# A head pair's block transpositions in its predecessor's fourth step, and one tile for the last keys' weights and inverses

## The chip, the cores and the metric

The kernel runs on one core of a Trainium2 chip. The metric is the device time of one execution in microseconds. Before the change three executions took 1657.55, 1662.69 and 1664.34 us; the median is 1662.69 us. The profile shows one execution with a span of 1655.7 us on the core.

## What is computed

Two blocks follow each other, all in fp32, for 8 batches of 576 tokens. The first is attention with 8 heads of 64 dimensions, in which only scores within tau of their row's maximum count:

```python
scores = scale * np.matmul(q, k.transpose(0, 1, 3, 2))
thresh = np.max(scores, axis=-1, keepdims=True) - tau
scores = np.where(scores >= thresh, scores, -1000000000.0)
attn = np.exp(scores - np.max(scores, axis=-1, keepdims=True))
attn = attn / (np.sum(attn, axis=-1, keepdims=True) + 1e-09)
out = np.matmul(attn, v)
```

The heads are then put side by side (576 x 512 for each batch), and the second block mixes and widens them:

```python
mixed = np.real(np.fft.fft(np.fft.fft(x, axis=1), axis=2))
u = x + mixed
un = (u - mean(u)) / np.sqrt(var(u) + 1e-06)
return u + np.maximum(un @ w_ch1, 0.0) @ w_ch2
```

The two channel weights (512 x 2048 and 2048 x 512) come as 64-bit floats and are converted to fp32 inside the kernel.

## The kernel before, in words

**Steps.** The attention works on pairs of heads, 4 pairs in each of 8 batches, so 32 pairs. A pair takes five steps (t = 0 to 4). In steps 0 to 3 both heads' scores for 128 queries are computed (`scores`, line 430, two score tiles of two PSUM banks each). In the fifth step (t = 4) the last 64 queries of both heads are done together from a block-diagonal tile `q_ends` (line 436), so that only one score tile is used. There are two buffers of score tiles in all. `softmax` then takes the maximum on VectorE (L453), the exponential on ScalarE (L461), and the masking with its sum on VectorE (L469), which is the last reader of a score tile. In the first two batches the weights are not normalized: `rec` holds the inverse of each sum, spread over 128 columns by GpSimd (L493).

**Weights transposed.** In the next step `transposed_weights` brings the previous step's weights to keys by queries: TensorE transposes them into PSUM (L533 the last 64 keys of both heads, L536 the inverses, both into one bank `pe`; L552 the other keys into `pw`), and ScalarE copies them out (L540 and L544 for `pe`, L554 and L556 for `pw`). The last keys' weights go to the tile `ends`, the inverses to the tile `recs`. `weighted_values` multiplies with v (L581) and, in the first two batches, with the inverses on VectorE (L589). For pairs whose heads are taken in reverse, GpSimd writes a reversed v (`v_rev`, L522 and L528) first.

**Preparing a pair.** q and k are loaded in 32-column pieces. `scale_q` (L390, GpSimd) scales q in place, and `prep_pair` transposes 32 by 32 blocks on VectorE: k (L401), a piece of k (L402) and q (L404), into `kT` (two buffers) and `qT` (one buffer), then issues the loads of the pair after it. `prep_ends` (L413, GpSimd) copies the last 64 queries from `qT` to `q_ends` at t = 1, so that after the scores of t = 3 nobody reads `qT` any more.

**Three stages of the program.** The order on the engines in the first two is the order in which the code is written.

- Batch 0 (`step`, 20 steps, until about 135 us): attention alone, beside the conversion of the first channel weight, whose passes lie on VectorE (L297, L300, L313), ScalarE (L305, L308, L311) and GpSimd (L318, L319). `busy` lets TensorE multiply dummy tiles.
- Batch 1 (`second_batch`, 20 steps, about 135 to 315 us): attention of batch 1, the conversion of the second channel weight, the Fourier mixing of batch 0 (the additions into `u_t`, L723 and L727) and the first channel products (L814 and L840), which `fill` puts between the attention's matmuls. `advance` runs the conversion's stages.
- Batches 2 to 7 (the last loop, from about 315 us): only TensorE's order is as written; a planner orders the other engines. Here `prep_pair` already stands at t = 3, and weights are normalized before they are transposed, so there are no inverses.

In the first two stages `prep_pair(n + 1)` stands at t = 4, after the softmax of that step. In `second_batch`, `prep_ends` and `scale_q` stand ahead of the mixing and of the transposed weights.

Of the kernel before, what the change touches and what calls it, by code (L numbers as in the profile page):

```python
# [9 lines left out]
FP32 = mybir.dt.float32  # L10
INT32 = mybir.dt.int32
UINT32 = mybir.dt.uint32
ALU = mybir.AluOpType
# [34 lines left out]
def kernel(  # L48
# [12 lines left out]
    nc = tc.nc  # L61
    B, H, S, D = q.shape
# [4 lines left out]
    NT = 5  # L67
# [341 lines left out]
    def prep_ends(n):  # L409

        for j in range(2):
            hp = slice(64 * j, 64 * j + 64)
            nc.gpsimd.tensor_copy(q_ends[hp, hp], heads[n][0][hp, 512:S])  # L413
# [90 lines left out]
    def weights_in_parts(i):  # L504

        n, t = divmod(i, NT)
        e, rec = steps.pop(i)
        if t in (0, 2):

            e_t = sb.tile([128, 8, S - 256], FP32, tag="e_t", bufs=1, name="e_t")
            ends = sb.tile([128, S - 256], FP32, tag="ends", bufs=1, name="ends")
            recs = None
            if rec is not None:
                recs = sb.tile([128, S - 256], FP32, tag="sums", bufs=1, name="recs")
            vt = heads[n][2]
            if t == 0 and PAIRS[n % NPAIR] % 2:

                vt = sb.tile([128, 10, D], FP32, tag="vr", bufs=1, name="v_rev")  # L520
                src = heads[n][2]
                nc.gpsimd.tensor_copy(vt[:, :, 0:1], src[:, :, 0:1])  # L522
                last = src[:, :, D - 1 : D]
                down = bass.AP(
                    tensor=last.tensor, offset=last.offset,
                    ap=[list(last.ap[0]), list(last.ap[1]), [-1, D - 1]],
                )
                nc.gpsimd.tensor_copy(vt[:, :, 1:D], down)  # L528
            heads[n] = (*heads[n][0:2], vt, e_t, ends, recs)
        e_t, ends, recs = heads[n][3:6]  # L530
        q0 = 128 * (t - (0 if t < 2 else 2))
        pe = ps.tile([128, 4, 128], FP32, tag="mm", bufs=4, name="pe")
        nc.tensor.transpose(pe[:, 0, :], e[:, 512:640], ident[:, :])  # L533
        kept = [ends]
        if rec is not None:
            nc.tensor.transpose(pe[:, 1, :], rec[:, :], ident[:, :])  # L536
            kept.append(recs)
        for c, dst in enumerate(kept):
            if t < 4:
                nc.scalar.copy(dst[:, q0 : q0 + 128], pe[:, c, :])  # L540
            else:
                for j in range(2):
                    hp = slice(64 * j, 64 * j + 64)
                    nc.scalar.copy(dst[hp, q0 : q0 + 64], pe[hp, c, hp])  # L544
        qs = slice(q0, q0 + (128 if t < 4 else 64))
        for j in range(2 if t < 4 else 1):
            pw = ps.tile([128, 4, 128], FP32, tag="mm", bufs=4, name="pw")
            if j == 1:
                yield
            for c in range(4):  # L550
                c0 = (S + D) * j + 128 * c
                nc.tensor.transpose(pw[:, c, :], e[:, c0 : c0 + 128], ident[:, :])  # L552
            if t < 4:
                nc.scalar.copy(e_t[:, 4 * j : 4 * j + 4, qs], pw[:, :, :])  # L554
            else:
                nc.scalar.copy(  # L556
                    e_t[:, :, qs].rearrange("p (j c) q -> p j c q", j=2),
                    pw[:, :, :].rearrange("p c (j q) -> p j c q", j=2),
                )

    def weighted_values(n, part):

        b, p = n // NPAIR, PAIRS[n % NPAIR]
        _, _, vt, e_t, ends, recs = heads[n]
        m = (256, S - 256)[part]
        if n % NPAIR == 0 and part == 0:

            xs[b] = [None] * NPAIR
            x = xs[b][p] = sb.tile([128, m], FP32, tag="half", bufs=1, name="x_first")
        else:  # L570
            x = xs[b][p]
            if x is None or n % NPAIR == 0:
                x = sb.tile([128, S], FP32, tag=f"x{p}", bufs=1, name=f"x{p}")
            if n % NPAIR == 0:
                nc.gpsimd.tensor_copy(x[:, 0:256], xs[b][p][:, :])
            xs[b][p] = x
        cols = slice(256 * part, 256 * part + m)
        pv = ps.tile([128, 512], FP32, tag="mm", bufs=4, name="pv")
        for c in range(5):
            for j in range(2):  # L580
                nc.tensor.matmul(  # L581
                    pv[64 * j : 64 * j + 64, 0:m], vt[:, 2 * c + j, :],
                    e_t[:, 4 * j + c, 0:m] if c < 4 else ends[:, 0:m],
                    start=(c == 0), stop=(c == 4), skip_group_check=True,
                )
        if normalized(n):
            nc.scalar.copy(x[:, cols], pv[:, 0:m])  # L587
        else:
            nc.vector.tensor_tensor(  # L589
                out=x[:, cols], in0=pv[:, 0:m], in1=recs[:, 0:m], op=ALU.mult  # L590
            )
        if part == 0:
            return
        heads.pop(n)
        if p % 2:

            swap = sb.tile([2, S], FP32, tag="half", bufs=1, name="swap")
            for j in range(2):
                nc.sync.dma_start(out=swap[j : j + 1, :], in_=x[64 * j : 64 * j + 1, :])
            for j in range(2):  # L600
                nc.sync.dma_start(out=x[64 * j : 64 * j + 1, :], in_=swap[1 - j : 2 - j, :])
# [575 lines left out]
    def step(i):  # L1177

        n, t = divmod(i, NT)
        scores(i)  # L1180

        def last_stages():
            run = chunks.pop(i - 1, None)
            for _ in range(2 if run else 0):
                next(run, None)

        if t == 1 and n > 0:
            softmax(i, lambda: weighted_values(n - 1, 1), last_stages)
            load_v(n + 1)
        elif t == 3:  # L1190
            softmax(i, lambda: weighted_values(n, 0), last_stages)
        else:
            softmax(i, None, last_stages)
        if t == 1 and n > 0:
            pass
        elif later and later[0][0] <= i:
            later.pop(0)[1](i)
        else:
            busy(2 if i < NCHUNK else 1)
        if t == 2:  # L1200
            scale_q(n + 1)
        if t == NT - 1:
            prep_pair(n + 1)
        if t == 1:
            prep_ends(n)
        if i in chunks:
            next(chunks[i])
        if i > 0:
            transposed_weights(i - 1)
        if i in chunks:  # L1210
            next(chunks[i])
        while after and after[0][0] <= i:
            after.pop(0)[1]()
        if i > 0 and i + 3 < NCHUNK:
            chunks[i + 3] = w1_chunk(i + 3)
        if t == 2 and n > 0:
            folds.append(fold_rows(n - 1))
        if folds and next(folds[0], True):
            folds.pop(0)
# [93 lines left out]
    def second_batch(i):  # L1313
# [10 lines left out]
        chunks.pop(first - 1, None)  # L1324
        transfers(first)
        fold_more()
        if t == 1:
            prep_ends(n)
        if t == 2:
            scale_q(n + 1)  # L1330
        if first == 0:
            weighted_values(n - 1, 1)
            scores(i + 1)
            column_means(LAST)
            copy_mean(LAST)
            folds.append(fold_rows(n - 1))
            while folds:
                fold_more()
            load_v(n + 1)
            start_batch(0)  # L1340
            mix(3)
            mix(3)
        elif first == 1:
            mix(3)
            transposed_weights(i - 1)
            mix(2)
            mirrored(LAST)
            for c, eng in ((1, nc.vector), (3, nc.vector), (0, nc.gpsimd), (2, nc.gpsimd)):
                less_mean(eng, LAST, c)
            advance(first)  # L1350
            advance(first)
        elif first == 2:
            mix(2)
            transposed_weights(i - 1)
            mix(2)
            weighted_values(n, 0)
            advance(first)
            advance(first)
        else:
            fill()  # L1360
            transposed_weights(i - 1)
            advance(first)
            advance(first)
            fill()
            if t == 4:
                prep_pair(n + 1)
            fill()
            if t == 2:
                weighted_values(n, 0)
            if t == 0:  # L1370
                weighted_values(n - 1, 1)
                folds.append(fold_rows(n - 1))
                load_v(n + 1)
        if first == 16:
            fold_halves(1)
        if first < 3:
# [96 lines left out]
```

## Time and profile before

| what | value |
|---|---|
| median of three executions | 1662.69 us |
| span in the profile | 1655.7 us |
| transposition of q (L404), 32 times | 0.76 to 0.78 us each |
| copies of `ends` and `recs`, 128 x 128 (L540), mean until 315 us | 0.264 and 0.273 us |
| copies of 64 x 64 (L544), mean until 315 us | 0.20 and 0.21 us |
| scaling of q on GpSimd (L390) around 210 to 300 us | 1.72 to 1.73 us |

The table's durations are those of single instructions, as the trace's groups and timelines give them. What a duration costs depends on whether another engine stands still meanwhile. In the lines of the profile, PE is TensorE, PEld its weight loads, DVE VectorE, ACT ScalarE, POOL GpSimd. A timeline's line has the start in us, the length in us, the engine, the line of the kernel, the operation, what it writes and reads, and how many instructions are merged in it; the square bracket at the end tells how long the engine stood idle before it and which instruction ended that. In the list of groups the columns are busy time, mean time of one in ns, and idle time before them with its main releaser.

### The profile page before, as it was taken

Reading aid. Unit: us, or ns where it says so; the run is one execution under the profiler, and the core shown is the slowest. Engines: PE = TensorE matmul, PEld = TensorE weight load, DVE = VectorE, ACT = ScalarE, POOL = GpSimd, SP = SyncE. Lnnn points to the kernel's source line nnn. Section 1 sums busy time; section 2 is a strip of 40 time slices with the busy share of each in tenths; the row PEclk is TensorE's granted clock in tenths of the full one; section 3 lists DMA queues with packets and bytes.
Section 4 is the critical chain, followed back from the end, with each engine's and each line's share of the span. In section 5 each row is a group of like instructions: output and inputs, shape, how many; then the busy total and the mean of one; then the engine's idle time right before and its main releaser. Section 6 shows DMA issues by size and latency. Waiting matters only on the chain.

```text
span 1655.7 us, 27993 instructions
## 1 busy us (share of the span) xinstructions
PE 1584.1 (96%) x10346; PEld 1248.7 (75%) x10346; DVE 1170.7 (71%) x2518; ACT 820.9 (50%) x1786; POOL 660.1 (40%) x875
## 2 busy tenths in 40 slices
PE   8888878999999999999999999999999999999998
PEld 4545445557888787878888778887888788889998
DVE  7986776667768678776676768787786868664444
ACT  5764566444535464645353556454646455532111
POOL 6773565141431525225333253424342244215232
PEclk9999989999999999999999999999999999999999
DMA  6423221211011111100101010111101110000000
GB/s 158 122 55 111 56 83 42 43 28 29 12 35 20 25 26 29 36 16 21 28 16 35 15 35 16 42 22 22 29 15 43 22 28 1 14 4 11 13 14 14
DMA packets 203086, 57.43 MB, mean 35 GB/s; under 512 B 193827, under 2 KB 193829, under 8 KB 202950
## 3 DMA queue, kind: packets, MB, share of 16 engines
q1 hardware_dynamic: 200438, 55.34, 14.2%
q8 instruction: 82, 1.34, 0.3%
q10 hardware_dynamic: 2512, 0.30, 0.1%
q14 instruction: 54, 0.44, 0.1%
HBM read 46.02 MB, written 9.44 MB: 33 GB/s over the span
## 4 chain that ended last, share of the span: by engine, by line
PE 77%; DVE 14%; ACT 5%; issue 2%; POOL 1%; DVEq 0%; ACTq 0%; POOLq 0%
PE ph L918 23%; PE po L1082 20%; PE pv L581 9%; PE sc L430 8%; PE pw L552 5%; PE po L840 3%; DVE e L469 3%; DVE neg L453 2%; PE ph L814 2%; ACT e L461 2%; PE sc L436 1%; PE py L684 1%; PE pn L774 1%; PE pa L701 1%; DVE hs L1043 1%
## 5 line engine op out<-in xcount | busy, mean ns | idle before, releaser
L453 DVE TENSOR_REDUCE neg<-sc 128x1 f32<-128x576 f32 x288 | 207.5, 749 | 174.2 <-PE sc L430 159.9
L461 ACT ACTIVATE e<-sc,neg 128x576 f32<-128x576 f32 x288 | 212.2, 737 | 229.1 <-DVE neg L453 228.7
L469 DVE SCALAR_TENSOR_TENSOR e<-sc,thr,e 128x576 f32<-128x576 f32 x288 | 229.5, 813 | 50.5 <-ACT thr L465 49.0
L1082 PE MATMUL po<-w,hs 128*128 128x256 f32 x1024 | 246.9, 384 | 0.0
L1082 PEld LDWEIGHTS po<-w,hs 128*128 128x128 f32 x1024 | 186.7, 191 | 33.9 <-issue 12.9
L430 PE MATMUL sc<-kT,qT 64*128 64x288 f32 x1024 | 169.3, 434 | 35.0 <-DVE qT L404 27.7
L918 PE MATMUL ph<-u_t,w 128*128 128x128 f32 x1536 | 187.0, 276 | 0.0
L918 PEld LDWEIGHTS ph<-u_t,w 128*128 128x128 f32 x1536 | 179.1, 192 | 5.0 <-issue 3.7
L552 PE MATMUL pw<-ident,e 128*128 128x128 f32 x1152 | 171.2, 276 | 8.0 <-ACT y_o L689 2.3
L554 ACT COPY e_t<-pw 128x512 f32<-128x512 f32 x256 | 148.7, 594 | 49.8 <-PE pw L552 49.5
L430 PEld LDWEIGHTS sc<-kT,qT 64*128 64x128 f32 x1024 | 93.8, 188 | 98.3 <-issue 35.2
L552 PEld LDWEIGHTS pw<-ident,e 128*128 128x128 f32 x1152 | 135.7, 142 | 27.3 <-issue 4.2
L927 DVE TENSOR_TENSOR hs<-ph,hs 128x512 f32<-128x512 f32 x160 | 106.9, 685 | 69.5 <-PE ph L918 53.8
L918 PE MATMUL ph<-t_u,s_w 128*128 128x128 f32 x1024 | 126.4, 277 | 2.2 <-POOL t_u L892 1.8
L918 PEld LDWEIGHTS ph<-t_u,s_w 128*128 128x128 f32 x1024 | 119.5, 192 | 7.7 <-issue 4.9
L1082 PE MATMUL po<-hs,s_tile 128*128 128x256 f32 x512 | 121.5, 381 | 0.0
L796 DVE SCALAR_TENSOR_TENSOR u<-po,rstd,u 128x256 f32<-128x256 f32 (+1 forms) x164 | 75.3, 483 | 63.9 <-PE po L1082 62.9
L488 ACT ACTIVATE e<-e,den 128x576 f32<-128x576 f32 x96 | 74.5, 776 | 75.7 <-DVE den L481 75.3
L1082 PEld LDWEIGHTS po<-hs,s_tile 128*128 128x128 f32 x512 | 94.1, 190 | 13.7 <-issue 2.5
L935 ACT ACTIVATE hs<-hs 128x512 f32<-128x512 f32 x112 | 69.2, 630 | 62.1 <-DVE hs L927 62.1
L614 POOL TENSOR_TENSOR half<-x 128x287 f32<-128x287 f32 x48 | 40.5, 865 | 115.6 <-ACT x L587 61.0
L1078 POOL TENSOR_TENSOR hs<-hs,s_tile 128x512 f32<-128x512 f32 x32 | 42.1, 1318 | 109.4 <-PE po L1082 86.5
(196 smaller groups left out, 2911.2 us busy)
## 6 DMA issues: line engine op xcount, KB each, us to landing
hs<-in_moe_w_ch_dram SPq DMA_DIRECT2D x23, 512.0 KB, 4.5
q_in<-in_q_dram SPq DMA_DIRECT2D x128, 72.0 KB, 2.4
out_dram<-u SPq DMA_DIRECT2D x36, 256.0 KB, 2.1
k_in<-in_k_dram SPq DMA_DIRECT2D x124, 72.0 KB, 2.3
v_in<-in_v_dram SPq DMA_DIRECT2D x64, 128.0 KB, 2.3
w<-in_moe_w_ch_dram SPq DMA_DIRECT2D x6, 512.0 KB, 3.7
stage<-in_moe_w_ch_dram SPq DMA_DIRECT2D x3, 512.0 KB, 3.5
v_in<-in_v_dram SPq DMA_DIRECT2D x64, 16.0 KB, 2.1
```

The source lines that it names most:

```text
L430: nc.tensor.matmul(sc[j][:, c, 0:HALF], qT[hp, 128 * t : 128 * t + 128], kT[hp, k0 + HALF * c : k0 + HALF * (c + 1)], start=True, stop=True,)
L453: nc.vector.tensor_reduce(out=neg[:, j : j + 1], in_=sc[j][:, :, 0:HALF], axis=AXIS_XY, op=ALU.max, negate=True,)
L461: nc.scalar.activation(out=ej, in_=sc[j][:, :, 0:HALF], func=ACT.Exp, bias=neg[:, j : j + 1], scale=1.0)
L469: nc.vector.scalar_tensor_tensor(out=ej, in0=sc[j][:, :, 0:HALF], scalar=thr[:, j : j + 1], in1=ej, op0=ALU.is_ge, op1=ALU.mult, accum_out ...
L488: nc.scalar.activation(out=e[:, S : 2 * S], in_=e[:, S : 2 * S], func=ACT.Copy, scale=den[:, 1:2])
L552: nc.tensor.transpose(pw[:, c, :], e[:, c0 : c0 + 128], ident[:, :])
L554: nc.scalar.copy(e_t[:, 4 * j : 4 * j + 4, qs], pw[:, :, :])
L581: nc.tensor.matmul(pv[64 * j : 64 * j + 64, 0:m], vt[:, 2 * c + j, :], e_t[:, 4 * j + c, 0:m] if c < 4 else ends[:, 0:m], start=(c == 0), ...
L796: nc.vector.scalar_tensor_tensor(out=u, in0=product, scalar=self.rstd[:, t : t + 1], in1=u, op0=ALU.mult, op1=ALU.add,)
L918: nc.tensor.matmul(banks[name][:, 128 * q : 128 * q + 128], left[c][:, 512 * part + 128 * q : 512 * part + 128 * q + 128], right[c], start ...
L927: nc.vector.tensor_tensor(out=to, in0=bank, in1=to if other is None else other, op=ALU.add)
L1082: nc.tensor.matmul(bank[:, 0 : DM // 2], left[p], right[p], start=start and p == 0, stop=p == NK - 1, skip_group_check=True,)
```

## The change

Three things are changed, and only the first two batches are touched by name.

- `prep_pair(n + 1)` stands at t = 3 instead of t = 4, in `step` and in `second_batch`. Its purpose is to have the next pair's q and k in place before the pair's last step ends. The loads that it issues move with it.
- In `second_batch`, `prep_ends` and `scale_q` stand at the end of a step instead of its middle, behind what the same step puts on GpSimd.
- `ends` gets a second half that takes the place of `recs`. One ScalarE copy takes both from the bank `pe`: 128 x 256 elements for t < 4, two of 64 x 128 for t = 4. The tile `recs` had shared its buffer with a sum tile of the channel products; it is gone. Where there are no inverses, the copy is as before.

```diff
-            ends = sb.tile([128, S - 256], FP32, tag="ends", bufs=1, name="ends")
-            recs = None
-            if rec is not None:
-                recs = sb.tile([128, S - 256], FP32, tag="sums", bufs=1, name="recs")
+            ends = sb.tile([128, 2, S - 256], FP32, tag="ends", bufs=1, name="ends")
...
-        kept = [ends]
+        kept = 1
         if rec is not None:
             nc.tensor.transpose(pe[:, 1, :], rec[:, :], ident[:, :])
-            kept.append(recs)
-        for c, dst in enumerate(kept):
-            if t < 4:
-                nc.scalar.copy(dst[:, q0 : q0 + 128], pe[:, c, :])
-            else:
-                for j in range(2):
-                    hp = slice(64 * j, 64 * j + 64)
-                    nc.scalar.copy(dst[hp, q0 : q0 + 64], pe[hp, c, hp])
+            kept = 2
+        if t < 4:
+            nc.scalar.copy(ends[:, 0:kept, q0 : q0 + 128], pe[:, 0:kept, :])
+        else:
+            for j in range(2):
+                hp = slice(64 * j, 64 * j + 64)
+                nc.scalar.copy(ends[hp, 0:kept, q0 : q0 + 64], pe[hp, 0:kept, hp])
...
@@ step
-        if t == NT - 1:
+        if t == 3:
             prep_pair(n + 1)
...
@@ second_batch
-        if t == 1:
-            prep_ends(n)
-        if t == 2:
-            scale_q(n + 1)
         if first == 0:
             weighted_values(n - 1, 1)
...
-            if t == 4:
+            if t == 3:
                 prep_pair(n + 1)
...
+        if t == 1:
+            prep_ends(n)
+        if t == 2:
+            scale_q(n + 1)
         if first == 16:
             fold_halves(1)
```

More of the change, by code (lines that the diff above doesn't have):

```diff
@@ L528, in weights_in_parts @@
                 nc.gpsimd.tensor_copy(vt[:, :, 1:D], down)
-            heads[n] = (*heads[n][0:2], vt, e_t, ends, recs)
-        e_t, ends, recs = heads[n][3:6]
+            heads[n] = (*heads[n][0:2], vt, e_t, ends)
+        e_t, ends = heads[n][3:5]
         q0 = 128 * (t - (0 if t < 2 else 2))
@@ L563, in weighted_values @@
         b, p = n // NPAIR, PAIRS[n % NPAIR]
-        _, _, vt, e_t, ends, recs = heads[n]
+        _, _, vt, e_t, ends = heads[n]
         m = (256, S - 256)[part]
@@ L582, in weighted_values @@
                     pv[64 * j : 64 * j + 64, 0:m], vt[:, 2 * c + j, :],
-                    e_t[:, 4 * j + c, 0:m] if c < 4 else ends[:, 0:m],
+                    e_t[:, 4 * j + c, 0:m] if c < 4 else ends[:, 0, 0:m],
                     start=(c == 0), stop=(c == 4), skip_group_check=True,
@@ L589, in weighted_values @@
             nc.vector.tensor_tensor(
-                out=x[:, cols], in0=pv[:, 0:m], in1=recs[:, 0:m], op=ALU.mult
+                out=x[:, cols], in0=pv[:, 0:m], in1=ends[:, 1, 0:m], op=ALU.mult
             )
```

## The prediction

> **What bounds the kernel now.** I read the page's busy times and slices first, then the table of stretches, then who waits for the transposition of q, then each boundary between two pairs in the timeline.
>
> ```profile
> span 1655.7 us, 27993 instructions
> ...
> PE 1584.1 (96%) x10346; PEld 1248.7 (75%) x10346; DVE 1170.7 (71%) x2518; ACT 820.9 (50%) x1786; POOL 660.1 (40%) x875
> ...
> PE   8888878999999999999999999999999999999998
> ...
> L430 PE MATMUL sc<-kT,qT 64*128 64x288 f32 x1024 | 169.3, 434 | 35.0 <-DVE qT L404 27.7
> ```
>
> TensorE is 96% busy, but slices 1 to 7 (some 290 us) are not full. The row of the scores names the largest wait of TensorE in the page: 27.7 us, all put down to the transposition of q.
>
> ```profile
> 0.00:135.00 135.00, 113.76 (x562) 64.72 (x562) 110.94 (x251) 88.35 (x197) 94.81 (x155) 0.98 0.41 105
> 135.00:315.00 180.00, 151.83 (x763) 90.97 (x764) 125.95 (x280) 99.44 (x229) 89.96 (x112) 0.93 0.27 72
> 315.00:1656.00 1341.00, 1318.52 (x9022) 1092.98 (x9020) 933.82 (x1988) 633.14 (x1361) 475.33 (x608) 1.00 0.10 23
> ```
>
> Columns after the length: TensorE, its weight loads, VectorE, ScalarE, GpSimd, granted clock. Up to 135 us (batch 0 of the attention) VectorE is at 111 of 135 us, TensorE partly runs dummy products. From 135 to 315 us (batch 1) TensorE idles 28 us and its clock is 0.93. After 315 us it is 98% busy, so what is won before 315 us should move the end one for one.
>
> ```profile
> 221.15 1.04 PE L552 MATMUL pw<-ident,e 128*128 128x128 f32 x8
> 230.66 2.29 PE L430 MATMUL sc<-kT,qT 64*128 64x288 f32 x8 [8.47 <-DVE qT L404]
> 232.88 4.51 PE L814 MATMUL ph<-u_t,w 128*128 128x384 f32 x8
> ...
> 223.99 0.82 DVE L469 SCALAR_TENSOR_TENSOR e<-sc,thr,e 128x576 f32<-128x576 f32 x1 [1.30 <-ACT thr L465]
> ...
> 228.79 0.77 DVE L401 STREAM_TRANSPOSE kT<-k_in 128x576 f32<-128x576 f32 x1
> 229.57 0.24 DVE L402 STREAM_TRANSPOSE kT<-k_in 64x64 f32<-64x64 f32 x1
> 229.82 0.78 DVE L404 STREAM_TRANSPOSE qT<-q_in 128x576 f32<-128x576 f32 x1
> ```
>
> The longest of the eight waits, in batch 1. TensorE is done at 222.19 us and can't start the next pair's scores until the transpositions end at 230.60, though the fifth step's masking (L469), the other thing it needs for a free score bank, ended at 224.8. Two integer passes of the weight conversion (L297, L300) stand between. Afterwards TensorE runs at about half speed (x8 of L814 take 4.51 instead of 2.75 us).
>
> ```profile
> 70.32 1.24 PE L430 MATMUL sc<-kT,qT 64*128 64x288 f32 x8 [2.96 <-DVE qT L404]
> ...
> 70.19 1.08 DVE L297 TENSOR_SCALAR w<-hs 128x512 int32<-128x512 int32 x1
> ...
> 164.84 1.92 POOL L390 TENSOR_SCALAR q_in<-q_in,q_scale 128x576 f32<-128x576 f32 x1
> ...
> 171.61 2.93 PE L814 MATMUL ph<-u_t,w 128*128 128x384 f32 x4 [3.59 <-POOL u_t L727]
> ```
>
> First row pair: in batch 0 VectorE goes straight on to L297, so TensorE's wait is not the bound there. Second pair: scaling q stands on GpSimd ahead of the six additions that make u_t, for which TensorE waits 3.59 us.
>
> [...] the transpositions above stand behind the conversion's passes, whose result TensorE doesn't need. [...] after the waits of 8.47, 3.59 and 3.35 us the clock was half, after 2.88 and 2.52 us it was not, after 3.03 and 0.83 us close together it was. [...] L300, one shape, takes 0.41 to 1.52 us; I treat it as noise of 1 us.
>
> **The change, part by part.**
>
> 1. *Transpositions in the fourth step instead of the fifth, eight pairs.* One set takes 0.77 + 0.24 + 0.78 = 1.79 us of VectorE in either place. Removed: the wait of the scores on them. What then ends last is L469 of the fifth step (it frees the second score bank). Added: 1.79 us on VectorE ahead of the fifth step's maximum (L453), its exponential and that same L469, unless VectorE was idle there.
>  - Batch 0, boundaries at 39.4, 70.3, 101.4 us: VectorE has no gap in the fourth step, L453 moves by 1.8 us, L469 too; the fifth step gets 1.8 us back. Left over is TensorE's head start: the scores' end before L453, some 0.2 to 0.3 us each. Sum 0.7.
>  - 132.27: VectorE idle 1.11 us before the fifth step's L453, so it moves by 0.73; L469 ends at 130.6 instead of 129.9, scores start there: gain 1.6. The values' products behind it wait for ScalarE's copies (item 2): 0.4 more. They run at half speed now (4.54 and 1.17 us against 2.37 and 0.71 in the next pair: 2.6 us lost); the wait falls from 3.03 to 1.5 us; I take half of 2.6. Sum 3.3.
>  - 185.94: VectorE was idle 5.28 us in the fourth step, cost nothing; L469 had ended at 182.0, TensorE was free at 183.06: the 2.88 us vanish for TensorE, 2.2 for ScalarE, which has a ReLU ending at 185.8 ahead of the exponential. I take 2.2.
>  - 230.66: L453 moves by 1.75, but the exponential waited for ScalarE until 222.97, so L469 moves by 0.5 and ends at 225.3: gain 5.3. Half speed cost 1.05 (2.29 against 1.24) and 1.76 (4.51 against 2.75); TensorE still idles 3.1 us, so I take only a quarter, 0.7. Sum 6.0.
>  - 270.60: the transpositions queue behind a reciprocal that waits until 263.69; L453 ends 1.8 later, the exponential was held by a table load until 265.34, so L469 moves by 1.0 and scores start at 268.3: 2.3. The idleness falls from 3.35 to 1.1 us, half speed goes (1.05 + about 0.3): 1.3. Sum 3.6.
>  - 305.04: VectorE was idle 1.67 us; L453 moves by 0.2, scores from 305.04 to 303.0. Sum 2.0.
> 2. *One copy for two.* 32 pairs of 128x128 copies (0.264 and 0.273 us) become 32 of 128x256. The 128x512 copy takes 0.60, so by straight line one takes 0.37; two back to back take 0.43 from start to end. Gain 0.06 each, hidden mostly behind the waits of ScalarE for L453 (35.4 us in batch 1). In the fifth step's copies four of 64x64 (0.86 us from 42.96 to 43.82) become two: 0.4 each, on the path only at 132 us (counted above). The joint copy now waits for the reader of the inverses as well (L589; 2.6 us in four cases already wait so for the second copy, right behind the first), so nothing new waits long.
> 3. *Scaling q and the small q copies go later on GpSimd, batch 1.* At 171.61 u_t comes 1.92 - 0.52 (the two L413 copies, which now lie in the same busy stretch) = 1.4 us earlier; half speed after it (x4 in 2.93 us; at the 2.75 us for x8 it would be 1.4) costs 1.5, of which I take 1.0. Sum 2.4. At 209.73 TensorE waits 1.86 us for v_rev behind L413: 0.5. q is still ready: scaled at about 172, transposed from 173.2; later pairs 259.7 against 263.8 and 295.2 against 298.
> 4. *Loads of q and k issued a step earlier.* Nothing waits for them in batch 1; nothing gained.
> 5. *After step 40* TensorE's order is unchanged and VectorE's moves in a few places near 320 us; cost none, within 1 us.
>
> Sum: 0.7 + 3.3 + 2.2 + 6.0 + 3.6 + 2.0 + 2.4 + 0.5 = 20.7. 1662.7 - 20.7 = 1642.0 us. Ends of it: without any clock recovered and each boundary 10 to 15% worse, 14 us (1649); with all half speed recovered and the 2.9 us whole, 26 us (1637).
>
> **The rivals.**
> - *The wait only moves* (12%): batch 1 acts like batch 0, L469 or the conversion behind it takes the place of the transpositions, and a third of item 1's boundaries after 132 us stays (13.4 / 3 = 4.5), with 0.7, 1.4 and 0.5: 7 us, 1655.5. For it: VectorE is 70% busy in batch 1 and the first three boundaries. Against it: its idle gaps of 5.28, 1.67 and 1.25 us just where the transpositions go.
> - *More than counted* (8%): all waits of batch 1 and all half speed go: 0.7 + 3.0 + 2.6 + 3.4 + 2.9 + 0.5 + 8.2 + 2.8 + 3.3 + 1.4 + 2.5 = 31 us, 1631. For it: the loads and the conversion run ahead. Against it: L469 of the fifth step at 224.8.
> - *Slower* (2%): the fifth step's L453 moves by 1.79 in seven boundaries, nothing comes back, and the different order after step 40 costs a little: 1662.7 + 12.5 = 1675. Only if the scores then waited for something I don't see.
>
> **How the numbers follow.** 78% for the forecast, 12, 8 and 2 for the rivals. The measurements of before spread from 1657.6 to 1664.3, so 3 us of the range are theirs. 80%: 1633 to 1652. Faster by over 0.5% is under 1654.4: the forecast, the second rival, and half of the first: 0.91; same 0.07; slower 0.02.
>
> **What would show it.** The row of L430 should lose "DVE qT L404" and wait for L469, some 5 us in all; the stretch from 135 us shorter by about 20; its clock 0.96 or more; the wait of L814 for u_t about 2.2 us. It is wrong if L453 of the fifth step now waits on the transpositions in batch 1 and TensorE's scores come no earlier, or if the stretch after 315 us is no longer of the same length.

## The result and the profile after

| | before | after |
|---|---|---|
| median of the executions | 1662.79 us (1657.55 to 1664.34, 4 executions) | 1635.03 us (1634.93 to 1635.14, 4 executions) |
| the profiled execution | 1657.55 us, span 1655.7 us | 1634.93 us, span 1632.8 us |

The ratio of the times is 0.9839, 95% interval 0.9817 to 0.9860: the changed kernel is faster by 27.8 us of the medians. In two later series, each with both kernels on one chip, the medians differ by 24.1 us (1659.84 and 1635.78 us) and by 26.5 us (1662.40 and 1635.86 us). The two profiled executions differ by only 22.6 us, which matters below.

The page of the changed kernel, its head, TensorE's 40 slices and the row of the scores:

```profile
span 1632.8 us, 27899 instructions
...
PE 1583.2 (97%) x10346; PEld 1247.7 (76%) x10346; DVE 1170.1 (72%) x2518; ACT 816.0 (50%) x1738; POOL 661.2 (40%) x875
...
PE   8998889999999999999999999999999999999998
...
L430 PE MATMUL sc<-kT,qT 64*128 64x288 f32 x1024 | 174.1, 433 | 11.0 <-DVE e L469 9.9
```

TensorE has the same 10346 products and the same busy time to 1 us; what went is idleness. The row of the scores has lost "DVE qT L404 27.7", and what releases it most is now L469, the masking that frees a score tile. ScalarE has 48 instructions fewer: the 32 pairs of copies became 32, and 32 small ones 16.

The same three stretches as before (length, then TensorE, its weight loads, VectorE, ScalarE, GpSimd, granted clock):

```profile
0.00:135.00 135.00, 121.45 (x584) 67.97 (x586) 109.82 (x258) 87.70 (x176) 95.83 (x155) 0.96 0.45 114
135.00:315.00 180.00, 164.85 (x848) 98.54 (x848) 141.60 (x312) 107.91 (x228) 89.69 (x112) 0.99 0.27 69
315.00:1632.00 1317.00, 1296.93 (x8919) 1081.14 (x8916) 918.70 (x1949) 620.35 (x1334) 475.64 (x608) 1.00 0.10 23
```

In the second row TensorE's idleness fell from 28.2 to 15.2 us and its clock rose from 0.93 to 0.99. In the first its clock fell from 0.98 to 0.96; whether the change has a price in batch 0 is taken up below. After 315 us fewer products are left, since the attention runs ahead.

Who TensorE waits for from 135 to 315 us (total, times, longest), some rows of before and then of the changed kernel:

```profile
PE sc L430 <- DVE qT L404: 17.2, 4, 8.5
...
PE ph L814 <- POOL u_t L727: 3.6, 1, 3.6
```

```profile
PE sc L430 <- DVE e L469: 2.6, 3, 1.9
PE ph L810 <- POOL u_t L723: 2.1, 1, 2.1
...
PE pv L577 <- POOL v_rev L525: 1.5, 1, 1.5
```

The transposition of q has fallen below these rows (0.9 us in two waits in all until 315 us); before, 17.2 of its 27.7 us lay in this stretch. The four pairs' steps from 132.3 us on (128.1 us in the changed kernel) take 18.7 us less than before, where the prediction looked for about 20. The boundary with the wait of 8.47 us now looks like this (timeline, TensorE, then VectorE):

```profile
209.35 1.04 PE L548 MATMUL pw<-ident,e 128*128 128x128 f32 x8
211.12 0.75 PE L430 MATMUL sc<-kT,qT 64*128 64x288 f32 x2 [0.73 <-DVE qT L404]
213.79 2.17 PE L430 MATMUL sc<-kT,qT 64*128 64x288 f32 x6 [1.92 <-DVE e L469]
215.89 3.53 PE L810 MATMUL ph<-u_t,w 128*128 128x384 f32 x8
...
210.29 0.78 DVE L404 STREAM_TRANSPOSE qT<-q_in 128x576 f32<-128x576 f32 x1
210.99 0.72 DVE L453 TENSOR_REDUCE neg<-sc 128x1 f32<-128x576 f32 x1
...
212.83 0.81 DVE L469 SCALAR_TENSOR_TENSOR e<-sc,thr,e 128x576 f32<-128x576 f32 x1
```

The transpositions stand directly ahead of the fifth step's maximum (L453) instead of behind its masking (L469) and the conversion passes (L297 and L300 twice each, four passes from 225.57 to 228.8 us before; the prediction spoke of two). The first two products of the scores start at once into a free tile, the other six wait for L469. TensorE is idle 2.65 us instead of 8.47.

### The profile page after: what moved, and what is told of

It reads as the page before. It is cut to its first block, busy times and chain, and to the rows that moved or that the text cites. A ratio compares the mean times of both kernels' runs of the same rounds, so it can differ in the third digit from the quotient of the medians.

```text
span 1632.8 us, 27899 instructions
## 1 busy us (share of the span) xinstructions
PE 1583.2 (97%) x10346; PEld 1247.7 (76%) x10346; DVE 1170.1 (72%) x2518; ACT 816.0 (50%) x1738; POOL 661.2 (40%) x875
## 4 chain that ended last, share of the span: by engine, by line
PE 76%; DVE 14%; ACT 5%; issue 2%; POOL 1%; DMA 1%; SPq 1%; DVEq 0%; ACTq 0%; POOLq 0%
PE ph L914 24%; PE po L1078 20%; PE pv L577 9%; PE sc L430 7%; PE pw L548 6%; PE po L836 3%; DVE e L469 2%; DVE neg L453 2%; ACT e L461 2%; PE sc L436 1%; PE ph L810 1%; PE py L680 1%; PE pa L697 1%; PE pn L770 1%; DVE hs L1039 1%
## 5 line engine op out<-in xcount | busy, mean ns | idle before, releaser
L453 DVE TENSOR_REDUCE neg<-sc 128x1 f32<-128x576 f32 x288 | 207.2, 747 | 165.4 <-PE sc L430 154.1
L469 DVE SCALAR_TENSOR_TENSOR e<-sc,thr,e 128x576 f32<-128x576 f32 x288 | 229.4, 812 | 49.5 <-ACT thr L465 48.0
L430 PE MATMUL sc<-kT,qT 64*128 64x288 f32 x1024 | 174.1, 433 | 11.0 <-DVE e L469 9.9
L548 PEld LDWEIGHTS pw<-ident,e 128*128 128x128 f32 x1152 | 134.3, 141 | 27.8 <-ACT y_o L685 4.2
```

The lines of the kernel that those rows point to most:

```text
L430: nc.tensor.matmul(sc[j][:, c, 0:HALF], qT[hp, 128 * t : 128 * t + 128], kT[hp, k0 + HALF * c : k0 + HALF * (c + 1)], start=True, stop=True,)
L453: nc.vector.tensor_reduce(out=neg[:, j : j + 1], in_=sc[j][:, :, 0:HALF], axis=AXIS_XY, op=ALU.max, negate=True,)
L469: nc.vector.scalar_tensor_tensor(out=ej, in0=sc[j][:, :, 0:HALF], scalar=thr[:, j : j + 1], in1=ej, op0=ALU.is_ge, op1=ALU.mult, accum_out ...
```

## What the trace says, boundary by boundary

The start of each step's scores, read off TensorE's timeline, shows where the time came from (step 0 is the first, step 20 begins at 132.3 us before). Each entry is the length of a stretch of steps in before's profile minus the same in the other's, in us (five steps a pair, 20 a batch; two more profiles of the changed kernel were taken with the experiments):

| steps | what lies there | predicted | after | second profile | third profile |
|---|---|---|---|---|---|
| 0 to 17 | first three boundaries of batch 0 | 0.7 | -1.0 | 0.6 | -3.1 |
| 17 to 18 | nothing of the change | 0 | 2.2 | 0.0 | 2.2 |
| 18 to 21 | boundary at 132 us | 3.3 | 4.1 | 4.5 | 4.1 |
| 21 to 24 | wait for u_t | 2.4 | 2.8 | 2.8 | 2.8 |
| 24 to 28 | boundary at 186 us, v_rev | 2.7 | 3.0 | 2.8 | 3.0 |
| 28 to 31 | boundary at 231 us | 6.0 | 5.5 | 5.5 | 5.5 |
| 31 to 36 | boundary at 271 us | 3.6 | 2.9 | 2.9 | 2.9 |
| 36 to 45 | boundary at 305 us | 2.0 | 1.9 | 1.9 | 1.9 |
| 45 to 155 | the rest | 0 | 0.3 | 0.0 | 0.0 |

From step 18 on the three profiles agree within 0.4 us, and the sum to step 45 is 20.2 us in the first one, where the prediction's terms make 20.0. In the steps 0 to 17 they differ by 3.7 us, of which 2.1 us are left at step 18 (1.2, 0.6 and -0.9 us ahead of before).

## The experiments

Ratios are to the kernel before in the same series. Transpositions alone, two copies, GpSimd's work in mid-step and the first timing of "batch 0 as before" come from one chip on which the changed kernel itself was not timed; the kernel before took 1657.74 us there in the median. A difference of 2 or 3 us between these four and the changed kernel's 1635.0 to 1635.9 us is therefore weak evidence by itself, and their traces count for more.

**Transpositions alone.** The kernel before with nothing but the two places of `prep_pair` changed.

```diff
-        if t == NT - 1:
+        if t == 3:
             prep_pair(n + 1)
...
-            if t == 4:
+            if t == 3:
                 prep_pair(n + 1)
```

> The kernel before with prep_pair at t = 3 in both early stages, and nothing else of the change. My theory (the wait of the scores on the transpositions was TensorE's in batch 1, and its half speed after it): all but the GpSimd order and the copies, so 1638 to 1640 us, 3 to 5 us over the changed kernel's 1635.0; the wait of L814 for u_t stays near 3.6 us, that for v_rev near 1.9. Rival (the three edits need each other, since scaling q ahead of u_t then delays the earlier transpositions): less than half of the gain, over 1649 us.

Measured 1640.76 us (1639.40 to 1642.08), ratio 0.9886 (0.9862 to 0.9910): 0.8 us above the forecast of 1638 to 1640, and far from the rival's 1649. Its waits from 135 to 315 us, with the line numbers of the kernel before:

```profile
PE ph L814 <- POOL u_t L727: 3.3, 1, 3.3
...
PE pv L581 <- POOL v_rev L528: 2.1, 1, 2.1
```

The waits for q are gone as in the changed kernel; those for u_t and v_rev are still there. By the stretches of the table from step 18 it has 4.2, then -0.2 at u_t, 2.9, 5.5, 2.4 and 1.9: every boundary, and nothing at u_t. So the transpositions carry 16.7 of the 20.2 us there. After step 45 this profile loses 1.3 us again; it has a stretch of half speed at 738 us. The loads of q and k move with the transpositions; their part was not tried alone, but no wait for a load stands among TensorE's waits from 135 to 315 us, before or after.

**Two copies.** The changed kernel with the inverses in their own tile again and one copy for each.

```diff
-            ends = sb.tile([128, 2, S - 256], FP32, tag="ends", bufs=1, name="ends")
+            ends = sb.tile([128, S - 256], FP32, tag="ends", bufs=1, name="ends")
+            recs = None
+            if rec is not None:
+                recs = sb.tile([128, S - 256], FP32, tag="sums", bufs=1, name="recs")
...
+        for c, dst in enumerate(kept):
+            if t < 4:
+                nc.scalar.copy(dst[:, q0 : q0 + 128], pe[:, c, :])
```

> The changed kernel, but with recs a tile of its own and two copies out of the bank, as before. My theory (the joint copy only matters where ScalarE's copies end last, at 132 us and in fifth steps): 0.3 to 1.2 us over the changed kernel, 1635.3 to 1636.2. Rival (ScalarE is on the path all through the first two batches): 0.06 us in 32 steps and 0.4 in 8, some 5 us, 1640.

Measured 1637.85 us (1637.31 to 1638.93), ratio 0.9872 (0.9852 to 0.9892): some 2 to 3 us over the changed kernel, more than the theory gave. The groups of ScalarE until 315 us, first of the changed kernel, then of this one (busy, mean ns, idle before):

```profile
L536 ACT COPY ends<-pe 128x256 f32<-128x256 f32 x32 | 11.8, 370 | 12.7 <-PE pe L533 7.2 <-PE pw L548 3.0 <-DVE x L585 1.5
```

```profile
L540 ACT COPY ends<-pe 128x128 f32<-128x128 f32 x34 | 9.0, 265 | 8.2 <-PE pe L536 8.2
L540 ACT COPY recs<-pe 128x128 f32<-128x128 f32 x32 | 8.8, 274 | 2.0 <-DVE x L589 1.9
```

The joint copy takes 0.370 us, the straight line of the prediction. In the trace the two kernels run about level until step 23 (from the first scores on, 5.0 us ahead of before in the changed kernel and 5.3 here). Then the one with two copies loses 1.7 us in one place, the products behind the wait for u_t:

```profile
165.08 2.63 PE L814 MATMUL ph<-u_t,w 128*128 128x384 f32 x4 [2.05 <-POOL u_t L727]
```

In the changed kernel the same four products take 1.56 us after the same wait (2.07 us). No copy is concerned: it is TensorE's clock, half from 165.41 to 168.83 us here and whole there. What is left for the copies is at most 0.6 us by step 36. Two copies aren't needed for that loss: in two profiles with the joint copy (the second of "batch 0 as before", and the one with three repeats below) half speed stands behind the same wait, and the stretch of steps 21 to 24 is 1.1 us ahead as here, not 2.8. Why all four executions here took longer than the trace explains isn't settled; that the direct gain of the joint copy is small is shown.

**GpSimd's work in mid-step.** The changed kernel with `prep_ends` and `scale_q` where they were.

```diff
+        if t == 1:
+            prep_ends(n)
+        if t == 2:
+            scale_q(n + 1)
         if first == 0:
             weighted_values(n - 1, 1)
...
-        if t == 1:
-            prep_ends(n)
-        if t == 2:
-            scale_q(n + 1)
```

> The changed kernel, but with prep_ends and scale_q in the middle of a second_batch step, as before. My theory: 1.4 us at u_t and 0.5 at v_rev come back as waits, with up to 1.5 us of half speed: 1637 to 1638.5 us. Rival (the earlier load of q and the other shifts hide it): within 0.5 us of 1635.0.

Measured 1638.99 us (1637.42 to 1639.60), ratio 0.9877 (0.9856 to 0.9897): 0.5 us above the forecast's range. Its waits from 135 to 315 us:

```profile
PE ph L810 <- POOL u_t L723: 3.3, 1, 3.3
...
PE pv L577 <- POOL v_rev L525: 2.1, 1, 2.1
```

Both waits are back (3.3 against 2.1 and 2.1 against 1.5 us), and the stretch of steps 21 to 24, 2.8 us ahead in the changed kernel, is at -0.2. So the 2.8 us there are the move on GpSimd, 1.2 to 1.5 us of wait and as much again of half speed behind it. The second part isn't certain in each execution: of the nine profiles with the work moved, six are 2.8 to 3.1 us ahead there, and three, with half speed behind the shorter wait too, only 1.1 us. In all four profiles with the old order half speed follows the wait. The stretch with v_rev has the same length in both (3.0 us ahead), so the 0.5 us of that wait are not seen at the end of it.

**Batch 1 as before, in the fifth step.** The changed kernel with the transpositions of batch 1 alone put back.

```diff
-            if t == 3:
+            if t == 4:
                 prep_pair(n + 1)
```

> The changed kernel, but batch 1 keeps the transpositions in the fifth step; batch 0 has them in the fourth. My theory (the gain of the transpositions lies in batch 1 alone, but for the boundary at 132 us): 2.2 + 5.3 + 2.3 + 2.0 us of waits and up to 5 us of half speed come back, 1647 to 1652 us. Rival (the waits only move, or ScalarE's and GpSimd's edits carry the gain): under 1643.

Measured 1651.06 us (1649.35 to 1654.07), ratio 0.9944 (0.9926 to 0.9963): within the forecast, and 15.3 us over the changed kernel on the same chip. Waits from 135 to 315 us, and the timeline of the boundary that lay at 231 us:

```profile
PE sc L430 <- DVE qT L404: 17.1, 4, 8.8
```

```profile
226.18 2.29 PE L430 MATMUL sc<-kT,qT 64*128 64x288 f32 x8 [8.77 <-DVE qT L404]
```

The old waits return with their old lengths, and steps 24 to 45 lose all of their 13.3 us. That puts the larger part of the gain in batch 1's four boundaries, against the rival by which the wait would only move to L469. Around the fifth steps there VectorE had idle time to take up the transpositions, ahead of the maximum at 186 and 305 us, behind it at 231 and 271 us, where it waits for ScalarE (1.30 us ahead of L469 at 223.99 us).

**Batch 0 as before.** The changed kernel with the transpositions of the first three pairs' successors back in the fifth step; the one before batch 1 stays in the fourth. It was run twice, the second time beside the changed kernel itself.

```diff
-        if t == 3:
+        if t == (3 if n == NPAIR - 1 else 4):
             prep_pair(n + 1)
```

> The changed kernel, but the first three pairs of batch 0 keep the transpositions in the fifth step; only the one at 132 us and batch 1 have them in the fourth. My theory, amended after the trace of the changed kernel (the scores of steps 12 to 17 start 0.3 to 1.2 us later than before, for VectorE has no gap there): 0.5 to 1.0 us less than the changed kernel, 1634.0 to 1634.5. As predicted at first (0.2 to 0.3 us gained at each of the three boundaries): 0.7 us more, 1635.7. Rival (batch 0 gains as batch 1 does): 5 us more, 1640.

> The changed kernel with the first three pairs of batch 0 back in the fifth step, once more beside the changed kernel, for the two were not timed side by side yet. In its trace steps 5 to 17 take 1.1 us less than in the changed kernel's; the changed kernel then wins 2.1 us between the scores of steps 17 and 18, where this one had a half-speed window over dummy products. My theory (that window is chance, the 1.1 us are not): 0.5 to 1.5 us under the changed kernel. Rival (the shorter wait at each boundary keeps the windows away): 1 to 3 us over it.

> The changed kernel once more, beside the kernels of this call. My theory: 1635.0 us as in its four runs before, with a spread under 1 us; the kernel before 1657.5 to 1664.6. Rival (its steady runs were one position of the clock's windows among several, and its profile happened to hold little half speed on the path): 1636 to 1639 us with a spread of 2 us, as its relatives show.

Measured 1638.44 us (1636.78 to 1639.39), then 1637.80 us (1635.62 to 1639.67) beside 1635.78 us (1635.27 to 1635.88) of the changed kernel. The theory that batch 0 is better off without the change isn't borne out by the times: both medians are above the changed kernel's, in the second series by 2.0 us, within the rival's 1 to 3, though one of the four executions beside it lies among its own. In the first profile steps 0 to 17 took 1.1 us less than in the changed kernel's first, in the second 4.3 us more than in the one beside it. The fastest of the second series ran at a mean clock of 0.998, the other three at 0.992 to 0.995.

The profiles tell what decides there. Six of them have exactly the changed kernel's code up to step 17. Steps 0 to 17 are 1.3 us ahead of before in the one without any half speed in these steps, 0.6 ahead with one grid length of it (3.41 us, see below), 1.0 and 2.0 behind with three, 3.1 behind with four and 4.2 behind with five. With the transpositions in the fifth step they are at most 0.1 us from before in the two without half speed, and 3.5 and 3.7 behind in the two with three and four lengths of it. (The two profiles with the transpositions in the fourth step and separate copies fit less well: 0.3 behind with one, 0.6 ahead with two.) So each length goes with about 1 us in this part, and their number changes between executions of the same code.

**Dummy products in the waits.** The kernel before with two calls more of `busy`, so that TensorE isn't idle while it waits for q at the end of the fifth steps.

```diff
+        if i == per_batch - 1:
+            busy(2)
...
+        if first in (4, 9, 14):
+            busy(2)
```

> The kernel before, with two dummy products each (1.9 us of TensorE at full speed) at the ends of steps 19, 24, 29 and 34, in the waits of 3.03, 2.88, 8.47 and 3.35 us for the transposition of q. The waits stay; only the idleness in them is cut. My theory (idleness lets the clock fall to half and 5 to 7 us of the gain are that): 3 to 7 us under the kernel before. Rival (half speed after a wait costs nothing on the path, or the dummies lengthen the waits): the same as before, or up to 3 us slower.

Measured 1657.94 us (1656.53 to 1662.68), ratio 0.9989 (0.9980 to 0.9999): 1.9 us won in the medians, less than expected. The profile shows a fault of the experiment:

```profile
225.84 3.46 PE L112 MATMUL pd<-ones 128*128 128x512 f32 x4 [3.31 <-ACT recs L540]
231.01 1.24 PE L430 MATMUL sc<-kT,qT 64*128 64x288 f32 x8 [1.71 <-DVE qT L404]
```

The dummies need a PSUM bank, and waited 3.31 us for the copy that frees one. The scores run at full speed all the same (1.24 us instead of 2.29), and the trace gains 2.7 us at that boundary; 3.1 us go again at step 40, where TensorE now has half speed from 301.3 to 308.1 us, and steps 0 to 17, whose code is unchanged, are 3.5 us behind. So half speed was worth some 2 to 3 us at that wait, as the prediction had it (2.8), but half-speed stretches elsewhere take it back.

**Where the half-speed stretches lie.** The granted clock of the ten profiles up to this point has one pattern: the half-speed stretches begin on a fixed grid of 3.41 us (before's at 116.79 us and at 536.63 us are 123 lengths of 3.413 us apart), whose phase differs from execution to execution (the changed kernel's first, at 39.80 us, lies 22.56 lengths ahead of before's), and those that follow full speed follow a stretch of the grid in which TensorE was busy for no more than about 0.62 of the time. The table of stretches on the grid, of before (TensorE's busy time is the second number after the length, the clock the last but two):

```profile
222.61:226.02 3.41, 0.00 (x0) 0.00 (x0) 2.04 (x7) 2.44 (x8) 3.33 (x3) 1.00 0.02 6
226.02:229.43 3.41, 0.00 (x0) 0.00 (x0) 3.41 (x5) 2.30 (x5) 2.15 (x3) 0.50 0.52 156
229.43:232.85 3.42, 2.19 (x8) 1.19 (x8) 1.15 (x3) 1.67 (x3) 0.00 (x0) 0.50 0.27 46
232.85:236.26 3.41, 3.41 (x8) 1.87 (x7) 3.28 (x6) 1.59 (x3) 1.11 (x1) 0.50 0.63 101
```

After the stretch with no product the clock is half; it stays half behind the stretches of 0 and 0.64 busy, and is whole again after a full one. In the changed kernel the stretch from 210.47 to 213.88 us has 0.84 us of products, and the next one is at half speed: the products at 213.79 us above, which lie in it, take 2.17 us. To test this, the changed kernel was given something to do in these waits that needs no bank: the first product of the next scores is made again into the same tile.

```diff
+                    for _ in range({5: 3, 10: 2, 30: 3}.get(i, 1) if c == j == 0 else 1):
                         nc.tensor.matmul(
                             sc[j][:, c, 0:HALF], qT[hp, 128 * t : 128 * t + 128],
```

> The changed kernel in which the first scores' product of a pair (64x288, two instructions, 0.75 us) is made again into the same free bank, twice more in front of the second batch-0 pair and of batch 1's third pair, once more in front of the third batch-0 pair: the waits for L469 there (1.61, 1.30, 1.92 us) are filled, nothing else changes. Read from ten profiles: half-speed stretches lie on a fixed grid of 3.41 us, and each follows a stretch of the grid in which TensorE was busy under about 0.6 of the time (18 of 18 under 0.40, 39 of 86 between 0.40 and 0.62, none of 4473 over it). Theory: the half-speed stretches at 40, 70 and 214 us go; each costs 1.7 us where TensorE is the bound, so 1.7 at 214 and up to 1.7 for the two in batch 0 together: 1631.5 to 1633.5. Rival: these stretches cost nothing that isn't lost elsewhere, or the repeats delay the other products: 1635 or more, within 1 us of the changed kernel.

> The same, in front of batch 1's third pair alone (the wait of 1.92 us for L469). Theory: the half-speed stretch at 214 us goes, 1.7 us less: 1633.3 to 1634.2, and in the trace the steps after that pair's first come earlier by 1 to 1.7 us against the changed kernel. Rival: 1635 to 1636, the stretch stays or its time is lost at the next wait.

> The changed kernel once more, on the same chip, for the two before: 1635.0 to 1635.9, and the half-speed stretch near 214 us again.

On one chip: all three places 1635.65 us (1635.28 to 1636.67), the one place in batch 1 1634.02 us (1633.76 to 1635.92), the changed kernel 1635.86 us (1635.50 to 1637.03). Filling all three brought nothing measurable, though in its profile the clock is whole at all three. Behind the place in batch 1 (line numbers are one higher in this kernel):

```profile
215.79 1.21 PE L431 MATMUL sc<-kT,qT 64*128 64x288 f32 x6 [0.95 <-DVE e L470]
216.92 2.85 PE L811 MATMUL ph<-u_t,w 128*128 128x384 f32 x8
...
220.73 0.33 PE L534 MATMUL pe<-ident,rec 128*128 128x128 f32 x1 [0.85 <-POOL rec L494]
```

The six scores take 1.21 instead of 2.17 us and the channel products 2.85 instead of 3.53, but TensorE then waits 0.85 us for the inverses on GpSimd, and 1.18 instead of 0.61 us for ScalarE's copy of the weights. From the first of these scores to the next step's it is 14.98 us, and 14.99 in the changed kernel: the half speed at 214 us costs nothing in these two profiles, because the other engines end last there. That is the rival of this experiment.

Filling the one place brought 1.8 us of the medians, the size that the theory gave, but two of its five executions (1635.15 and 1635.92 us) lie among the changed kernel's. The profile is of the first of those two:

```profile
211.24:214.65 3.41, 2.06 (x9) 1.40 (x11) 3.34 (x9) 2.23 (x7) 1.61 (x2) 1.00 0.59 125
214.65:218.06 3.41, 3.41 (x9) 1.78 (x6) 3.41 (x4) 2.08 (x5) 3.33 (x3) 0.50 0.52 81
```

With 2.06 of 3.41 us busy (0.60) the next stretch still went to half speed. In the three profiles of this series half speed followed every stretch under 0.40, about half of some 20 from there to 0.62, and one of more than 1350 above (at 0.63), much as in the ten before. So the pattern held. What made three executions faster wasn't seen; by the profile of the three places it isn't the half speed at 214 us, and their mean clock, 0.995, is no higher than the changed kernel's 0.994 to 0.996.

## Why the prediction was right, and where its terms were off

- **What bounds, and what replaces it.** Right: the wait for the transposition of q is gone from the row of the scores, and L469 is the releaser. The row waits 9.9 us for it, not "some 5 us in all", because L469 already held up 6.6 us of other scores until 315 us in before's trace, which that sentence left out; 2.6 us of it lie in batch 1.
- **Item 1, batch 0: +0.7 predicted, 0.6, -1.0 and -3.1 in three profiles.** The step that failed is that the term counted time on VectorE alone, without TensorE's clock. At the first boundary six of the eight scores start 0.5 us earlier; 0.15 of that is the earlier start of the fifth step (32.70 against 32.85 us), which leaves the 0.3 that were reckoned. But their first two products go ahead alone and the wait of 1.61 us comes after them, and the next stretch of the grid is at half speed. First the changed kernel, then before:

```profile
36.58 0.75 PE L430 MATMUL sc<-kT,qT 64*128 64x288 f32 x2
38.93 1.47 PE L430 MATMUL sc<-kT,qT 64*128 64x288 f32 x6 [1.61 <-DVE e L469]
40.33 3.40 PE L112 MATMUL pd<-ones 128*128 128x512 f32 x4
```

```profile
39.41 1.24 PE L430 MATMUL sc<-kT,qT 64*128 64x288 f32 x8 [2.62 <-DVE qT L404]
40.58 1.98 PE L112 MATMUL pd<-ones 128*128 128x512 f32 x4
```

  The four dummies take 3.40 instead of 1.98 us and hold back the next transposed weights. Before's profile had no such stretch until 116.8 us, although TensorE waited longer there: with 0.51 to 0.62 busy in stretches at the three boundaries it was in the zone where either happens. In this part of the kernel the number of such stretches decides over up to 5 us, as the profiles under "batch 0 as before" show.
- **132 us: 3.3 predicted, 4.1 to 4.5.** The term took half of the 2.6 us of half speed; all of it came back. The sixteen products of the values, before and then in the changed kernel:

```profile
135.45 4.54 PE L581 MATMUL pv<-e_t,v_in 128*64 128x320 f32 x16 [0.83 <-ACT e_t L556]
```

```profile
132.03 2.37 PE L577 MATMUL pv<-e_t,v_in 128*64 128x320 f32 x16 [0.79 <-ACT e_t L552]
```

- **231 us: 6.0 against 5.5; 271 us: 3.6 against 2.9; 305 us: 2.0 against 1.9; 186 us and v_rev: 2.7 against 3.0.** The method (idle time in the fifth step's chain absorbs the transpositions, L469 ends last) held to within 0.7 us each. At 231 us no half speed could be won: it stayed at the scores (2.17 us for the last six) and at the channel products behind them, and where it was filled, other engines ended last. The 2.7 us in the fourth place hide two errors: the 0.5 us for v_rev are not seen in the stretch, and the boundary at 186 us gives 2.9 us where 2.2 were counted.
- **u_t: 2.4 predicted, 2.8 measured** in the first profile and, with the move on GpSimd undone, nothing. The 2.8 hold 1.5 us less of wait (2.07 against 3.59 us) and about 1.3 us of clock. Three of the nine profiles with the work moved lack the clock's part; the mean of the nine is 2.3 us. The half-speed terms were the author's estimates from the length of each wait. The length alone doesn't decide: half speed already followed stretches of the grid that were half busy, after 1.6 us of continuous idleness (1.80 of 3.41 us busy from 36.39 us on, changed kernel), and at 198.7 us of before's own profile, which the prediction's list of waits leaves out, behind waits of 1.04 and 0.73 us (busy 0.48 of the stretch).
- **The joint copy:** nearly hidden, as costed (0.4 us on the path); at most 0.6 us in the trace, the clock apart.
- **After step 45:** 0.0 to 0.3 us, as costed.
- **The sum was right, the base was not.** The profiled executions differ by 22.6 us, the terms sum to 20.7. That they come so near is in part luck: the errors at 132 and 186 us and at u_t have the opposite sign of those at v_rev, 231 and 271 us, and batch 0 and u_t differ from profile to profile (0.6 to -3.1 us; 1.1 to 3.1 us with the work moved). The prediction subtracted them from the median of 1662.7 us, but had worked them out on an execution of 1657.55 us. The missing 5 us are before's own spread. In 27 executions of it in one series the six shortest (1655.54 to 1657.73 us) had mean clocks of 0.986 to 0.990, the five longest (1663.98 to 1665.78 us) 0.982 to 0.984: by these clocks the longer ones hold more half-speed time. The changed kernel, with the long waits gone, ran at 0.993 to 0.996 in its twelve executions. So the gain in the median very likely contains half-speed time that the profiled execution of before didn't have, and that no single trace could show; no execution of before near its median was profiled to see where it lies. The time lies between the forecast and the rival "more than counted" (1631 us), but not for that rival's reason: the waits that it lets vanish in batch 1 are still there (u_t 2.1, v_rev 1.5, L469 2.6 us).
- **A slip in the sums.** The boundaries after 132 us add up to 13.8 us (2.2, 6.0, 3.6 and 2.0), not to the 13.4 of the first rival; a third of them is 4.6, and its time stays near 1655.5 us.

## What to carry to other kernels

Where the trace shows an engine's instructions queueing one behind the other, as VectorE's transpositions did here behind four conversion passes (225.57 to 228.8 us) while TensorE waited 8.47 us for them, ask for each instruction what waits behind it: work for the next stage belongs ahead of the current stage's last chain, where that chain has idle time to take it up, and not behind its end. The instruction that then ends last can be read from the trace of before. When a wait is removed, count the half-speed time behind it as well, and treat it as a quantity that varies between executions (here by up to 5 us in batch 0): subtract a gain that is read in a profile from the time of that profiled execution. Before filling a wait to keep the clock, ask whether TensorE ends last behind it: at 214 us here it didn't, and the whole clock brought nothing. A filler that needs what the waited-for chain holds waits itself, as the dummies did here for a PSUM bank (3.31 us).

## What the runs showed of the hardware that was not expected

- Half-speed stretches of TensorE begin on a grid of 3.41 us that is fixed within an execution, in all thirteen profiles. In the first ten, of the stretches run at full speed, those under 0.40 busy were followed by half speed in 18 of 18 cases, from 0.40 to 0.62 in 39 of 86, above that (the limit was read off these profiles) in none of more than 4400. What decides between 0.40 and 0.62 stays open.
- The same wait of 2.0 to 2.1 us for u_t was followed by half speed in three of nine profiles and then cost 1.7 us more; the wait of 2.9 us at 183 us of before was not followed by it.
- The same kernel before ranges over 10 us (1655.5 to 1665.8 us), and its time follows its mean clock (0.990 to 0.982).
